# The sixth expert of a routed mixture, too, in products of two parts of each operand

## The chip, the cores and the metric

The kernel runs on one core of a Trainium2 chip. Its five engines work side by side, each through its own list of instructions: TensorE (PE; its weight loads are shown apart, as PEld), VectorE (DVE), ScalarE (ACT), GpSimd (POOL), and SyncE (SP), which here issues nearly all transfers between main memory and the core. The metric is device time of one launch in microseconds, median of several runs.

## The reference, cut to what matters

```python
x = attention(q, k, v)                    # 4 batches, 12 heads, 448 tokens, 64 wide -> [1792, 768]
logits = x @ w_gate                       # 8 experts
# greedy: in falling order of logits each token goes to its expert, 224 tokens per expert
for e in range(8):
    h = np.maximum(x[assigned == e] @ w1[e], 0.0)   # [224, 768] @ [768, 1024]
    out[assigned == e] = h @ w2[e]                  # [224, 1024] @ [1024, 768]
gate = 1 / (1 + np.exp(-(out @ w_gate2)))           # 768 -> 1536
final = (gate * (out @ w_val2)) @ w_out2            # 1536 -> 768
```

All of it is float32. The second, gated layer follows the experts.

## The kernel before, in words

Three stages follow each other: attention, the experts with the routing, the gated layer. The experts are worked in the order in which the routing closes them. A *phase* `ph` (0 to 7) is one round of the routing: it finds the next expert that is full, its number (`ei[ph]`) and the 224 rows that it gets (`ids[ph]`). `moe(ph, nxt)` then multiplies that expert; the sixth expert is `ph` = 5.

**One expert.** `xprep` turns the gathered rows with 12 TensorE transposes (L820). The first product has four chunks of `w1`, each 256 columns wide: 12 products of a 128x128 weight block with 224 columns, so 48 in all. The second product has four chunks of `w2` and also 48. A hidden chunk is taken out of PSUM by ScalarE (L862), and in a split expert its low part by VectorE (L864). All matrix products are issued at L778.

**Plain and split.** For a phase that isn't in `SPLIT` operands are float32 and each product is one matmul, which the trace shows as two records of PE. For a phase in `SPLIT` every operand has a high part (rounded to the type `fp32r`) and a low part (the rest), and a product is three matmuls: high·high, high·low, low·high (`prod` inside `moe`). The low part of the turned rows is made by L825.

**Weights.** Chunks are loaded in the order of use by `load_chunk` into a ring of 8 buffers, tile `w`. A chunk is fetched in two halves of 384 KB (`load_half`: L762 for `w1`, L768 for `w2`). A plain chunk takes one buffer, and the transfer writes into it, so that it can't start before TensorE has finished with what lay there. A split chunk takes two buffers. Its transfers go into one of four staging tiles, `raw`; then per half ScalarE writes the high part (L689) and VectorE the low part (L690). So a transfer into `raw` waits for a staging tile, and L689 and L690 wait for TensorE to leave the buffers.

**Routing.** `route()` runs beside the experts, one phase ahead of need or more. A phase is a chain of short steps between VectorE and TensorE. Six times VectorE compares (L498), TensorE counts with 14 short matmuls (L503), VectorE tests the counts (L514, tile `ge`), TensorE spreads them (L516), and VectorE narrows the search. Then come a prefix sum (L574, L577, read by TensorE at L580), the one-hot rows (L615), the count of the indices by TensorE (L619), and the indices themselves (L621, L622). SP stores them at L624 in tile `idx_d`, 224 words of 4 bytes each, and POOL gathers the rows of the next expert (L803). `tick` and `step` put these steps among the expert's matmuls at fixed places, by a count of the matmul time that has passed.

**What sets the order.** TensorE's order is that of the code. The lists of the other engines are laid out ahead of time by a scheduler that simulates the program; routing steps have priority. On the chip each engine works through its list.

**Weights of the gated layer.** They are float64 words in memory and are converted by a chain of ScalarE and VectorE steps (L83 to L94, tiles `cs`, `ca`, `sq`). The first two pieces of them are converted while the fifth expert runs.

The body of `load_chunk` for a split chunk:

```python
wh_, wl_ = wt(), wt()
for n in range(2):
    cc = slice(n * 768, (n + 1) * 768)
    raw = mo.tile([128, 768], F32, name="raw", bufs=4)
    load_half(kind, a, c, n, raw)
    nc.scalar.activation(wh_[:, cc], raw, AF.Copy)
    nc.vector.tensor_tensor(wl_[:, cc], raw, wh_[:, cc].bitcast(F32), op=OP.subtract)
```

Of the kernel before, what the change touches and what calls it, by code (L numbers as in the profile page):

```python
# [21 lines left out]
E = 8  # L22
# [8 lines left out]
def body(ctx: ExitStack, tc: tile.TileContext, q, k, v, moe_w_gate, moe_w1, moe_w2,  # L31
# [635 lines left out]
    for f in range(0, NF, 2):  # L667
        chunks += [("s0", 1, f), ("s1", 1, f), ("wo", 1, f)]

    SPLIT = (E - 2, E - 1)  # L670
    W = {}
    stream = {"next": 0}
    regs = {}
# [2 lines left out]
    def wt(dt=F32R):  # L676
        return mp.tile([128, CH], dt, name="w", bufs=WB)

    def load_chunk():
        kind, a, c = chunks[stream["next"]]  # L680
        if kind in ("w1", "w2") and a not in regs:
            regs[a] = nc.sync.value_load(ei[a][0:1, 0:1], min_val=0, max_val=E - 1)
        if kind in ("w1", "w2") and a in SPLIT:
            wh_, wl_ = wt(), wt()
# [125 lines left out]
    def xprep(ph):  # L810
        xs = XE[ph]
        sp = ph in SPLIT
        xx = mo.tile([128, KD, CAP], F32R if sp else F32, name="xx", bufs=2)
# [16 lines left out]
    def moe(ph, nxt):  # L830
        xx = XE[ph]
        hs_ = []
        sp = ph in SPLIT

# [239 lines left out]
```

## Time and profile before

| | us |
|---|---|
| median of 3 runs | 1130.82 |
| lowest, highest | 1128.95, 1131.06 |
| the profiled execution, its own time | 1130.21 |
| its span in the trace | 1128.4 |
| PE busy | 1076.9 (95%) |
| DVE busy | 699.1 (62%) |
| ACT busy | 439.5 (39%) |
| POOL busy | 270.2 (24%) |
| TensorE's granted clock, mean share | 0.979 |

Times in the trace are microseconds from the start of the span. The profiled execution's own time is 1.8 us longer than the span and 0.6 us under the median. Attention lasts to about 247, the opening of the routing to 283, the experts from there to 602, and the gated layer to the end. A busy share tells how long an engine had something in it, not that it decided the time; what decides is read from who waited for whom.

### The profile page before, as it was taken

How to read it: one execution, taken by the hardware profiler on the slowest of the kernel's cores; microseconds unless marked ns; L12 is line 12 of the kernel's file. 1: busy time of each engine (PE TensorE's matmuls, PEld its weight loads, DVE VectorE, ACT ScalarE, POOL GpSimd, SP SyncE). 2: the span in 40 equal slices, each digit the busy share in tenths (PEclk: the TensorE clock that was granted, in tenths of full speed). 3: DMA queues.
4: the chain of work that ended last, by engine and by line, in shares of the span. 5: the costliest groups of instructions: out<-in, count | busy, mean ns of one | idle time of the engine just before them, and what ended most of it. 6: DMA issues, size and time to landing. Idle time of an engine off the chain costs nothing.

```text
span 1128.4 us, 19849 instructions
## 1 busy us (share of the span) xinstructions
PE 1076.9 (95%) x7401; PEld 1020.8 (90%) x7401; DVE 699.1 (62%) x1980; ACT 439.5 (39%) x846; POOL 270.2 (24%) x371
## 2 busy tenths in 40 slices
PE   6999999982999999999999899999999999999997
PEld 6999999971899999999999799999999899899897
DVE  5777777766555556442557989878736515435535
ACT  4767677730111111123454465543414442322310
POOL 7333333300000000000000300000125746546522
PEclk9999999995999999999999899999999999999999
DMA  8556565525687667786747676655311521220212
GB/s 173 121 124 170 117 166 122 145 82 97 228 197 193 128 178 193 165 210 181 226 154 226 240 250 229 236 169 191 93 81 56 183 87 54 97 99 29 85 57 98
DMA packets 156991, 167.26 MB, mean 148 GB/s; under 512 B 74576, under 2 KB 140128, under 8 KB 156640
## 3 DMA queue, kind: packets, MB, share of 16 engines
q1 hardware_dynamic: 153472, 154.74, 46.1%
q0 software_dynamic: 2496, 11.04, 5.3%
q8 instruction: 58, 0.95, 0.4%
q10 hardware_dynamic: 928, 0.23, 0.1%
q14 instruction: 37, 0.30, 0.1%
HBM read 122.32 MB, written 32.64 MB: 137 GB/s over the span
## 4 chain that ended last, share of the span: by engine, by line
PE 90%; DVE 5%; issue 1%; DMA 1%; POOL 1%; ACT 1%; POOLq 0%; SPq 0%; ACTq 0%; DVEq 0%
PE g L778 67%; PE o L348 8%; PE w L328 4%; PE s L295 3%; PE s L296 2%; PE r L503 2%; PE w L257 1%; PE g L820 1%; DMA x_d<-x2f 1%; PE w L386 1%; PE w L369 1%; DVE ca L89 1%; DVE w L94 1%; DVE ca L92 0%; DVE hx L934 0%
## 5 line engine op out<-in xcount | busy, mean ns | idle before, releaser
L778 PE MATMUL g<-xq,w 128*128 128x448 f32 x1188 | 282.1, 367 | 0.0
L778 PEld LDWEIGHTS g<-xq,w 128*128 128x128 f32 x1188 | 222.7, 188 | 21.4
L778 PE MATMUL g<-w,hx 128*128 128x384 f32 x1008 | 181.6, 338 | 7.9 <-DVE hx L934 5.8
L778 PEld LDWEIGHTS g<-w,hx 128*128 128x128 f32 x1008 | 176.4, 190 | 12.0 <-DVE hx L934 8.3
L778 PE MATMUL g<-xx,w 128*128 128x224 f32 x768 | 151.4, 339 | 0.0
L778 PE MATMUL g<-hx,w 128*128 128x224 f32 x864 | 151.2, 331 | 0.0
L778 PEld LDWEIGHTS g<-hx,w 128*128 128x128 f32 x864 | 137.6, 191 | 2.5 <-issue 1.0
L778 PEld LDWEIGHTS g<-xx,w 128*128 128x128 f32 x768 | 134.9, 191 | 2.2 <-issue 0.2
L778 PE MATMUL g<-xs,w 128*128 128x448 f32 x432 | 124.7, 365 | 0.0
L742 POOL TENSOR_TENSOR w<-cs,w 128x384 fp32r<-128x384 f32 x84 | 84.2, 1024 | 121.4 <-ACT w L741 121.3
L348 PE MATMUL o<-vt,pt 112*112 112x65 f32 x960 | 106.3, 258 | 0.0
L348 PEld LDWEIGHTS o<-vt,pt 112*112 112x112 f32 x960 | 101.9, 178 | 0.0
L923 DVE TENSOR_TENSOR acc<-g,acc 128x384 f32<-128x384 f32 x140 | 75.3, 554 | 33.3 <-PE g L778 32.3
L298 DVE CUSTOM_DVE_ANT_0 sm<-s,mask 112x112 f32<-112x112 f32 (+1 forms) x192 | 78.4, 445 | 23.0 <-PE s L296 23.0
L306 ACT ACTIVATE sm<-sm,mn 112x112 f32<-112x112 f32 (+1 forms) x192 | 90.3, 522 | 5.1 <-DVE mn L298 5.1
L778 PEld LDWEIGHTS g<-xs,w 128*128 128x128 f32 x432 | 81.1, 188 | 6.2
L803 POOL DMA_INDIRECT xg<-x_d,ids x16 | 15.4, 962 | 296.3 <-DVE ids L622 105.4
L268 POOL CAST st<-hi 64x448 fp32r<-64x448 f32 x96 | 53.3, 556 | 133.4 <-ACT hi L263 122.8
L741 ACT ACTIVATE w<-cs 128x384 fp32r<-128x384 f32 x84 | 40.0, 518 | 92.4 <-PE g L778 48.7
L295 PE MATMUL s<-st,st 128*112 128x112 f32 (+1 forms) x192 | 62.2, 339 | 3.0 <-POOL st L268 2.6
L328 PE MATMUL w<-ident,sm 112*112 112x112 f32 x480 | 62.7, 261 | 0.1
L296 PE MATMUL s<-lo,qz 128*112 128x112 f32 (+1 forms) x192 | 56.5, 309 | 0.0
(214 smaller groups left out, 1450.0 us busy)
## 6 DMA issues: line engine op xcount, KB each, us to landing
w<-in_moe_w_dram SPq DMA_DIRECT2D x96, 384.0 KB, 6.6
raw<-in_moe_w_dram SPq DMA_DIRECT2D x32, 384.0 KB, 4.6
cs<-in_moe_w_gate_dram SPq DMA_DIRECT2D x12, 768.0 KB, 4.2
cs<-in_moe_w_val_dram SPq DMA_DIRECT2D x12, 768.0 KB
wsc<-ca SPq DMA_DIRECT2D x24, 384.0 KB, 4.7
cs<-in_moe_w_out_dram SPq DMA_DIRECT2D x12, 768.0 KB, 4.2
wsc<-w SPq DMA_DIRECT2D x12, 768.0 KB, 4.0
cs<-wsc SPq DMA_DIRECT2D x24, 384.0 KB, 3.1
```

The lines of the kernel that those rows point to most:

```text
L268: nc.gpsimd.tensor_copy(st[r, h], hi[r].bitcast(F32))
L295: nc.tensor.matmul(ss[j], qq[:, j, qs], kh[:, j, :w], start=True, stop=False)
L296: nc.tensor.matmul(ss[j], QZ[u % NZ][:, j, qs], kl[:, :w], start=False, stop=True)
L298: nc.vector.tensor_tensor_reduce(sm[:, j, :w], ss[j], mask[:, S - w:], op0=OP.add, op1=OP.min, scale=1.0, scalar=3.0e38, accum_out=mn[:, j ...
L306: nc.scalar.activation(sm[:, j, :w], sm[:, j, :w], AF.Exp, bias=mn[:, j:j + 1], scale=-1.0)
L328: nc.tensor.transpose(w[:P, n, :], sm[:, j, c * P:(c + 1) * P], ident[:P, :P])
L348: nc.tensor.matmul(o[:, n, j, :], pt[:, j * (i + 1) + c, :], vt[:, j, c, :], start=c == 0, stop=c == i)
L503: nc.tensor.matmul(c[:, :J], oha[:, tt_, :], cmps[2 * tt_ // T][:, tt_ % (T // 2), :J], start=tt_ == 0, stop=tt_ == T - 1)
L741: nc.scalar.activation(hi, src, AF.Copy)
L742: nc.gpsimd.tensor_tensor(lo, src, hi.bitcast(F32), op=OP.subtract)
L778: nc.tensor.matmul(o, a, b, start=first, stop=last_)
L923: nc.vector.tensor_tensor(ac, po[:, :384], ac, op=OP.add)
```

## The change

One line: the sixth expert (phase 5) joins the two that are split already.

```diff
-    SPLIT = (E - 2, E - 1)
+    SPLIT = (E - 3, E - 2, E - 1)
```

The names in the lists below are the lines and tiles that were described above; a count behind `x` stands for equal neighbours. On VectorE, inside phase 6 of the routing, while the fifth expert's first product runs: the second search's first compare (`cmp`) and its test (`ge`).

```order
 L535 SCALAR_TENSOR_TENSOR key_6780<-hs,th,lo_152 128x14
 L498 TENSOR_TENSOR cmp<-key_6780,jc_64_1024_93 128x448 x2
+L690 TENSOR_TENSOR w<-raw,w 128x768 x2
 L514 TENSOR_SCALAR ge<-r,rem_129 128x64
 L519 TENSOR_SCALAR jk,acc<-r 128x64
```

The two low parts of the sixth expert's first chunk now stand between the compare and the test.

On VectorE a little later, at the prefix sum of phase 6 (`sc`, `tot`), which stands among conversion steps of the gated layer (`ca`):

```order
-L87 TENSOR_SCALAR ca<-cs 128x768
+L690 TENSOR_TENSOR w<-raw,w 128x768
 L574 SCALAR_TENSOR_TENSOR sc<-chain,pr 128x28
+L690 TENSOR_TENSOR w<-raw,w 128x768
 L87 TENSOR_SCALAR ca<-cs 128x768
 L591 SCALAR_TENSOR_TENSOR rem_129<-e_6964,d_115 8x1
 L564 SCALAR_TENSOR_TENSOR jk_7037,na<-ob,n_107 128x8
-L88 SCALAR_TENSOR_TENSOR ca<-cs,ca 128x768
+L87 TENSOR_SCALAR ca<-cs 128x768
 L577 CAST tot<-sc 128x2
```

The second chunk's two low parts now stand ahead of `tot`, and one conversion step (L88) has moved behind it.

On VectorE from the end of phase 7 of the routing (`ids`) on, through the sixth expert, as it stands now; before, nothing stood between `o` and `c`, and no L864 belonged to this expert:

```order
L615 TENSOR_TENSOR o_80<-pm,colp 128x7x112 x2
L825 TENSOR_TENSOR xl<-g,xx 128x448 x3
L690 TENSOR_TENSOR w<-raw,w 128x768 x2
L621 COPY c_7174<-r 112x4
L622 SCALAR_TENSOR_TENSOR ids_147<-c_7174 112x2
L690 TENSOR_TENSOR w<-raw,w 128x768 x2
L864 SCALAR_TENSOR_TENSOR hx<-g,hx 128x448
```

The first L690 pair here is the sixth expert's fourth chunk, the second its fifth, and L864 is its first hidden chunk. After these rows a pair and an L864 take turns three more times (chunks six to eight, hidden chunks two to four), so that each hidden chunk's low part comes behind the split of a later chunk of weights. ScalarE's list (L689 and L862) alternates in the same way.

SP issues as many transfers as before. The four halves of the sixth expert's first two chunks stand at the same place, behind the last half of the fifth expert's `w2`, but go into `raw`; the third chunk's two halves follow at once, too, and the fourth chunk's come behind the read of `ei` of phase 6. The index store of phase 6 (`idx_d`) now stands between the sixth expert's fifth and sixth chunk, and that of phase 7 between its sixth and seventh. PE's list differs in the sixth expert alone: 96 products become 288 matmuls. POOL's list is the same.

## Rows read from the trace of the kernel before

**Rows 1.** The page's first part: busy us, share of the span, instructions.
```profile
PE 1076.9 (95%) x7401; PEld 1020.8 (90%) x7401; DVE 699.1 (62%) x1980; ACT 439.5 (39%) x846; POOL 270.2 (24%) x371
```
**Rows 2.** Waits of PE, 300 to 620 us: us in total, times, longest.
```profile
PE r L516 <- DVE ge L514: 0.3, 1, 0.3
PE r L619 <- DVE o L615: 0.2, 1, 0.2
```
**Rows 3.** Timeline of PE, experts six to eight: start us, us, engine, line, count.
```profile
498.99 2.43 PE L778 MATMUL g<-xx,w 128*128 128x224 f32 x12
501.25 0.49 PE L619 MATMUL r<-r,o 128*128 128x4 bf16 x14
517.58 15.30 PE L778 MATMUL g<-hx,w 128*128 128x224 f32 x80
536.75 0.43 PE L778 MATMUL g<-xx,w 128*128 128x224 f32 x1
552.98 13.56 PE L778 MATMUL g<-hx,w 128*128 128x224 f32 x120
570.23 0.28 PE L778 MATMUL g<-xx,w 128*128 128x224 f32 x1
```
**Rows 4.** Groups by line and shape: count, busy us, mean ns, idle before.
```profile
L690 DVE TENSOR_TENSOR w<-raw,w 128x768 fp32r<-128x768 f32 x32 | 29.3, 956 | 42.1 <-ACT w L689 40.4 <-PE g L778 1.6
L689 ACT ACTIVATE w<-raw 128x768 fp32r<-128x768 f32 x32 | 25.5, 839 | 29.8 <-PE g L778 15.6 <-DMA raw<-in_moe_w_dram 14.2
```
**Rows 5.** Timeline of all engines, phase 6: compare, count, test, spread.
```profile
466.82 0.62 DVE L498 TENSOR_TENSOR cmp<-key,jc 128x448 bf16<-128x448 f32 x1
...
468.10 0.57 PE L503 MATMUL r<-cmp,oha 128*128 128x64 bf16 x14
...
468.71 0.28 DVE L514 TENSOR_SCALAR ge<-r,rem 128x64 bf16<-128x64 f32 x1 [1.27 <-PE r L503]
...
469.35 0.19 PE L516 MATMUL r<-ge,sv 128*128 128x64 bf16 x1
```
**Rows 6.** Timeline of SP, the issues at the fifth expert's start.
```profile
455.09 0.33 SPq L624 DMA_DIRECT2D idx_d<-ids  x1
455.68 2.34 SPq L768 DMA_DIRECT2D w<-in_moe_w_dram  x4
```
**Rows 7.** Tile w, SP at 457.64 us: the last of those four halves, us to landing.
```profile
L768 SPq DMA_DIRECT2D w<-in_moe_w_dram x1: 373/373/373, 457.6 to 457.6; - x1
DMA to landing us min/median/max: 16.0/16.0/16.0
```
**Rows 8.** Busy time by stretch; the last three columns are granted clock, DMA share, GB/s.
```profile
455.00:464.00 9.00, 9.00 (x73) 8.57 (x72) 4.02 (x18) 1.26 (x3) 1.86 (x2) 1.00 0.67 41
516.00:524.00 8.00, 8.00 (x44) 8.00 (x43) 2.09 (x3) 2.67 (x6) 0.00 (x0) 1.00 0.56 67
524.00:527.00 3.00, 3.00 (x17) 3.00 (x17) 0.08 (x1) 1.77 (x3) 0.00 (x0) 1.00 0.97 338
```
**Rows 9.** Timeline of SP: the index store of phase 7.
```profile
509.06 1.41 SPq L624 DMA_DIRECT2D idx_d<-ids  x1
```
**Rows 10.** Timeline of ACT: the seventh expert's first two halves.
```profile
513.35 0.84 ACT L689 ACTIVATE w<-raw 128x768 fp32r<-128x768 f32 x1 [8.64 <-DMA raw<-in_moe_w_dram]
514.43 0.84 ACT L689 ACTIVATE w<-raw 128x768 fp32r<-128x768 f32 x1 [0.24 <-DMA raw<-in_moe_w_dram]
```
**Rows 11.** Timeline of PE in the gated layer: a wait.
```profile
634.84 1.01 PE L778 MATMUL g<-w,hx 128*128 128x384 f32 x2 [2.00 <-ACT hx L933]
```
**Rows 12.** Busy time by stretch, columns as in rows 8, soon after that wait.
```profile
637.70:641.70 4.00, 4.00 (x12) 4.00 (x13) 3.06 (x5) 3.16 (x5) 0.00 (x0) 0.50 0.79 269
```
**Rows 13.** Timeline of all engines, phase 6: the prefix sum.
```profile
480.17 0.94 DVE L88 SCALAR_TENSOR_TENSOR ca<-cs,ca 128x768 uint32<-128x768 uint32 x1
...
481.04 0.15 DVE L577 CAST tot<-sc 128x2 bf16<-128x2 f32 x1
...
481.31 0.17 PE L580 MATMUL r<-tot,before 128*128 128x2 bf16 x1
```

## The prediction

> **What bounds the kernel now.** I read the page's busy shares first: PE is busy for 1076.9 of the span's 1128.4 us [rows 1]. A busy share proves nothing by itself, so I read next who PE waits for in the experts. From 300 to 620 us there are two waits, together 0.5 us, both for a routing step of DVE [rows 2]. So PE's list sets the time there. What PE saves comes off the end, and any wait put into its list is added in full. The timeline of PE prices the experts, the groups by line price the new work of ACT and DVE, and the timelines of the single engines, together with SP's issues and the table of stretches, tell when the new work's inputs are there.
>
> **The change part by part.**
>
> *PE's products.* The sixth expert runs from 498.99 to 536.75, that is 37.76 us plain; the seventh, split, from 536.75 to 570.23, that is 33.48 us [rows 3]. Both have 96 products and 12 transposes. The sixth also has 14 matmuls of the routing, busy for 0.49 us [rows 3], of which I count 0.36 on the path. Split, it should take 33.84 us: **-3.9 us**. The single products agree: 40 plain ones in 15.30 us are 0.38 us each, 40 split ones in 13.56 us are 0.34.
>
> The Trainium skill ("FP8 and Floating Point Precision", section TensorE Precision Notes) has true FP32 as four passes through the array. Three products in place of four passes would then save a quarter of 96 x 0.38, or 9.2 us. The rows disagree, since a split product costs 0.88 of a plain one and not 0.75, and the rows decide.
>
> *More splitting.* The expert has 8 chunks, so 16 halves: 16 x 0.839 = 13.4 us more on ACT and 16 x 0.956 = 15.3 us more on DVE [rows 4], and on DVE also three L825 and four L864. Neither engine is full there, so the sum costs nothing by itself. What costs is where it stands. DVE works its list in order, and two places of that list are inside the routing, for which PE waits.
>
> The Trainium skill says of this ("TensorE: Matmul & The Clock Gate", the table ahead of its first section) that ScalarE's and VectorE's queues are strictly first in, first out, while TensorE's may pull weight loads ahead. If that didn't hold on DVE, the next term would vanish and the gain of 3.9 us would stand. No run here tests it by itself.
>
> *First place, the test `ge` of phase 6.* Before, the compare is issued at 466.82, PE counts at 468.10, `ge` runs at 468.71 for 0.28 us, and PE's L516 follows at 469.35 [rows 5]. Now two L690 stand ahead of `ge`. They need both halves of the sixth expert's first chunk in `raw`, and L689 of each. When do those arrive? SP issues them right behind the four halves of the fifth expert's `w2` that go out from 455.68 on [rows 6]. The last of these four is issued at 457.64 and takes 16.0 us to land, so until 473.6 [rows 7]. The reason is in the table of stretches: in the 9 us after the index store of 455.09 the DMA engines are 67% busy and move only 41 GB/s [rows 6, 8]. The same follows the store of phase 7, issued at 509.06 behind other transfers: 67 GB/s for 8 us from 516 on, then 338 GB/s [rows 8, 9]. There the gather of rows is not near, so I put it down to the store. It is in the changed kernel at the same place.
>
> At 338 GB/s a half (384 KB, 0.393 MB) takes 1.16 us. The seventh expert's first two halves came 1.08 us apart, too [rows 10]. So the two halves land at about 474.8 and 475.9. L689 of the second ends at 476.8, L690 at 477.7, `ge` at 478.0, and L516 starts at about 478.15 in place of 469.35: **+8.8 us** of PE waiting. Bounds: if the halves were there, L690 could start at 468.1, when PE leaves the second buffer; 2 x 0.956 and `ge` end at 470.3, and PE waits 1.1 us. If they come 2 us later than I think, it is 11. I take 8.8, since the landing of that half is a row and not a guess. Behind the wait on DVE are all later steps of the routing, and on ACT the fifth expert's hidden chunk, which nobody needs that early.
>
> *The clock.* In the gated layer PE waited 2.00 us [rows 11]; afterwards the granted clock was 0.50, 1.2 GHz, and stayed there through 4.0 us of dense work from 637.70 to 641.70 [rows 12]. So the long wait should drop the clock as well, and about 4 us at half speed lose **+2.0 us** (bounds 0 and 2.0).
>
> *Second place, the prefix sum of phase 6.* DVE has no pause there. `tot` starts at 481.04 for 0.15 us, and PE's L580 at 481.31, 0.12 us later than `tot` ends [rows 13]. Two L690 (1.91 us) now come ahead of `tot` and one L88 (0.94) falls behind it [rows 4, 13], so it comes 0.97 us later: **+0.85 us** of waiting (bounds 0 and 1.9).
>
> *Inside the sixth expert.* The seventh and eighth run through without a wait [rows 2], with the same pattern of loads. The sixth has two index stores among its loads, and the one of phase 7 stands just ahead of the seventh chunk. Count from the expert's start. The store leaves at about 7 us, behind the sixth chunk, which phase 6's store has already delayed; the stretch of few bytes lasts to 15 [rows 8]. The seventh chunk's halves, 1.16 us each and partly moved by then, land at 16 to 16.5. Two L689, the take-out of the third hidden chunk behind them (0.5) and on DVE L690 and L864 (0.6) end at 19.2. PE finishes the first product after 16.2 us [rows 3] and wants that hidden chunk four products later, at 17.8: **+1.4 us**. Bounds: 0, as in the seventh expert, and 5.2 if the stretch lasts 9 us as from 455 on, nothing gets through in it, and the clock falls once more. I take 1.4.
>
> *After the sixth expert* the lists are those of before and every load waits for PE to leave a buffer, so all of it moves along: 0.
>
> *Sum.* -3.9 + 8.8 + 2.0 + 0.85 + 1.4 = **+9.1 us**. Against the profiled execution's own 1130.21 us that gives 1139.3. The median of the runs is 0.6 higher, within their spread, so I say 1139.5. With all low bounds: -3.9 + 1.1 = -2.8. With all high ones: -3.9 + 11 + 2 + 1.9 + 5.2 = +16.2.
>
> **Rivals.**
>
> *The halves are there in time (not slower).* This rests on one arrival: the first chunk in `raw` before 468. For it: the transfers no longer wait for PE and are issued as early as 458. Against it: they queue behind a transfer that landed at 473.6 [rows 7]. Then the two places cost 1.1 + 0.85 and the sum is -2.0, about 1128.5. It turns from slower to faster when the arrivals move ahead by some 6 us.
>
> *No wait at all (faster).* If DVE's extra work also fitted into the 1.27 us that it sat idle ahead of `ge` [rows 5], and the slack at `tot` sufficed, the whole -3.9 would come through: 1126.5. Against it: two L690 take 1.91 us.
>
> *The arrival lies between.* With the chunk there at 470 to 472, PE waits 3 to 5 us, the clock may hold, and the sum is -2 to +2: about 1131.
>
> *The columns alone set a product's price.* Three products of 224 columns would then cost three quarters of a plain one, and the 96 would save a quarter of 96 x 0.38, or 9.2 us; with the waits the sum is about +4, without them -9. The split experts' rows speak against it [rows 3]. The passes of the skill's page, above, give the same.
>
> *The sixth expert starves.* If each of its later chunks waits for a store, PE waits several times and the clock stays low: over +16, above 1146. For it: two stores in one expert with half the lead in weights. Against it: chunks five and six are issued well ahead.
>
> That the change doesn't do what it says is out: PE's list has three matmuls per product there.
>
> **How the numbers follow.** Forecast 0.72 (1133 to 1146 by itself). In time 0.10, half of it faster, half too small to tell. No wait 0.06. In between 0.05, no change. Columns alone, without waits, 0.02. Starving 0.05. What a measurement of this kernel can tell from no change is 0.2%, 2.3 us. So faster 0.13, same 0.10, slower 0.77. The range from 1129 to 1146 leaves out about half of "in time", the faster cases and the starving: just under 0.2.
>
> **What would show it.** In the changed kernel's trace: L516 after the first count of phase 6's second search with a wait of about 9 us for `ge`; on DVE L690 waiting for L689, and on ACT L689 for the transfer into `raw`; granted clock 0.50 just behind; a wait of about 1 us at L580; the sixth expert about 33.8 us long apart from waits, and one wait for L864 early in its second product; from the seventh expert on, rows as before, only later. I am wrong if the first L690 of the sixth expert finds its data, or if its products don't take 0.34 us each.

## The result, and the profile after

The changed kernel takes 1138.58 us (median of 6 runs, 1135.9 to 1140.26), the kernel before 1131.18 us in the 6 runs beside it and ahead of it (1128.95 to 1132.03). The ratio is 1.0063, its 95% interval 1.0046 to 1.0080: 7.4 us slower. The profiled execution took 1138.94 us, its span is 1137.2.

PE's busy time in the page of the changed kernel stands against [rows 1]:

```profile
PE 1074.7 (95%) x7497; PEld 1018.2 (90%) x7497; DVE 718.0 (63%) x2003; ACT 453.0 (40%) x862; POOL 269.9 (24%) x371
```

PE is busy for 2.2 us less than before and ends 8.7 us later. So the loss is waiting, and the next view is that of PE's waits from 300 to 640 us (columns: total, times, longest), where before had 0.5 us in all [rows 2]:

```profile
PE r L516 <- DVE ge L514: 7.7, 2, 7.4
PE g L820 <- DMA xg<-x_d,ids: 1.1, 1, 1.1
PE g L778 <- DVE hx L864: 0.7, 1, 0.7
PE r L580 <- DVE tot L577: 0.6, 1, 0.6
PE g L778 <- ACT hx L862: 0.4, 1, 0.4
```

The second line is a wait for the second expert's rows, ahead of anything that the change touches. With it and with what went before, the fifth expert starts 2.19 us later than in the profile of before. In the twelve other profiles below that start lies 0.9 to 7.3 us later than there, with the order of work up to it unchanged (one of them has the kernel before's own split). So it is scatter between executions, and in all tables here shifts are counted from the start of the fifth expert.

PE's timeline shows the two places in the routing, and then the sixth expert's second product; to set beside [rows 3, 5, 13]:

```profile
470.29 0.57 PE L503 MATMUL r<-cmp,oha 128*128 128x64 bf16 x14
479.14 0.21 PE L516 MATMUL r<-ge,sv 128*128 128x64 bf16 x1 [7.43 <-DVE ge L514]
493.61 0.18 PE L580 MATMUL r<-tot,before 128*128 128x2 bf16 x1 [0.64 <-DVE tot L577]
527.49 1.50 PE L778 MATMUL g<-hx,w 128*128 128x224 f32 x12
529.42 0.37 PE L778 MATMUL g<-hx,w 128*128 128x224 f32 x1 [0.43 <-ACT hx L862]
530.52 12.21 PE L778 MATMUL g<-hx,w 128*128 128x224 f32 x107 [0.73 <-DVE hx L864]
```

What DVE and ACT did meanwhile (DVE's three rows first, then ACT's; the wait ahead of a row stands in brackets):

```profile
468.47 1.16 DVE L498 TENSOR_TENSOR cmp<-key,jc 128x448 bf16<-128x448 f32 x2
477.05 1.84 DVE L690 TENSOR_TENSOR w<-raw,w 128x768 fp32r<-128x768 f32 x2 [7.42 <-DMA raw<-in_moe_w_dram]
478.80 0.28 DVE L514 TENSOR_SCALAR ge<-r,rem 128x64 bf16<-128x64 f32 x1
```

```profile
476.17 1.73 ACT L689 ACTIVATE w<-raw 128x768 fp32r<-128x768 f32 x2 [10.54 <-DMA raw<-in_moe_w_dram]
```

PE had finished counting at 470.9. `ge` takes 0.28 us, but two L690 stand ahead of it in DVE's list, and they wait for halves that ACT could first touch at 476.17. SP's issues and the table of stretches (last three columns: granted clock, DMA share, GB/s) tell why these come late, as [rows 6, 8] did:

```profile
457.29 0.33 SPq L624 DMA_DIRECT2D idx_d<-ids  x1
457.88 2.34 SPq L768 DMA_DIRECT2D w<-in_moe_w_dram  x4
460.40 10.31 SPq L762 DMA_DIRECT2D raw<-in_moe_w_dram  x4
```

```profile
457.30:466.00 8.70, 8.70 (x72) 8.28 (x71) 3.89 (x16) 1.26 (x3) 1.86 (x2) 1.00 0.68 35
470.00:478.80 8.80, 1.70 (x21) 1.36 (x20) 1.75 (x2) 2.12 (x3) 0.00 (x0) 0.83 0.93 278
479.10:483.00 3.90, 3.86 (x17) 3.44 (x17) 1.35 (x6) 0.00 (x0) 0.00 (x0) 0.54 0.64 201
```

For 8.7 us behind the index store the DMA engines move 35 GB/s. In the second row PE is busy for 1.7 of 8.8 us; in the third, the dense work behind the wait, the granted clock is mostly 0.50, that is 1.2 GHz.

How far each event of PE has moved against before, in us, counted from the fifth expert's start (for each kernel the profiled execution; "first spread" is the L516 behind the late `ge`, "after search" the search's last L516, "prefix" phase 6's L580):

| kernel | first spread | after search | prefix | sixth starts | seventh starts | eighth starts | end | ratio of the runs |
|---|---|---|---|---|---|---|---|---|
| changed kernel | +7.6 | +9.3 | +10.1 | +9.6 | +7.5 | +7.3 | +6.5 | 1.0063 |
| e6_late: no stores in the experts | +1.2 | +1.2 | +2.0 | +1.6 | -2.3 | -1.1 | -2.8 | 0.9988 |
| e3_store: the same, another late place | +1.6 | +1.6 | +2.4 | +1.9 | -1.9 | -1.2 | +7.3 | 1.0048 |
| x2_double: one store twice | +15.7 | +17.2 | +18.0 | +17.5 | +17.1 | +16.9 | +16.9 | 1.0173 |
| e7_before_late: before without the stores | -0.1 | -0.1 | -0.1 | -0.1 | -0.1 | -0.1 | -2.5 | 0.9998 |
| p1_products: no low parts of weights | 0.0 | 0.0 | 0.0 | +0.5 | -2.8 | -3.0 | -3.3 | 0.9979 |
| e1_pool: four L690 on POOL | 0.0 | 0.0 | +5.4 | +5.2 | +5.8 | +6.8 | +7.0 | 1.0055 |
| e1a_pool_first: two L690 on POOL | +0.3 | +0.3 | +4.3 | +3.8 | +3.5 | +3.3 | +3.4 | 1.0036 |
| e9_tot: L690 behind `tot` | +0.1 | +0.1 | +0.1 | +6.5 | +4.8 | +5.0 | +5.5 | 1.0057 |
| e8_late_tot: e6 and e9 | +0.1 | +0.1 | +0.1 | +6.7 | +2.9 | +3.4 | +3.2 | 1.0049 |
| e2_behind: L690 behind the row numbers | -0.1 | -0.1 | -0.1 | +5.0 | +7.0 | +6.9 | +5.9 | 1.0082 |
| e6b_late_behind: e6 and e2 | -0.1 | -0.1 | -0.1 | -0.2 | +1.0 | +2.4 | +6.2 | 1.0000 |
| e10_pauses: e6, L690 in DVE's pauses | 0.0 | 0.0 | 0.0 | +0.1 | -3.8 | -3.3 | -3.1 | 0.9985 |

### The profile page after: what moved, and what is told of

The parts are those of the page before. It is cut to its first block, busy times and chain, and to the rows that moved or that the text cites. A ratio compares the mean times of both kernels' runs of the same rounds, so it can differ in the third digit from the quotient of the medians.

```text
span 1137.2 us, 20102 instructions
## 1 busy us (share of the span) xinstructions
PE 1074.7 (95%) x7497; PEld 1018.2 (90%) x7497; DVE 718.0 (63%) x2003; ACT 453.0 (40%) x862; POOL 269.9 (24%) x371
## 4 chain that ended last, share of the span: by engine, by line
PE 86%; DVE 5%; DMA 5%; POOL 1%; issue 1%; ACT 1%; SPq 0%; POOLq 0%; DVEq 0%; ACTq 0%
PE g L778 63%; PE o L348 8%; PE w L328 4%; PE s L295 3%; PE s L296 2%; DMA xg<-x_d,ids 2%; DMA raw<-in_moe_w_dram 2%; PE w L257 2%; PE r L503 1%; PE g L820 1%; DMA x_d<-x2f 1%; PE w L386 1%; PE w L369 1%; DVE ca L89 1%; DVE w L94 1%
## 5 line engine op out<-in xcount | busy, mean ns | idle before, releaser
L778 PEld LDWEIGHTS g<-xx,w 128*128 128x128 f32 x768 | 133.0, 193 | 10.1 <-issue 7.7
L690 DVE TENSOR_TENSOR w<-raw,w 128x768 fp32r<-128x768 f32 x48 | 44.2, 955 | 40.5 <-ACT w L689 33.0
```

Source lines behind the costliest of these rows:

```text
L778: nc.tensor.matmul(o, a, b, start=first, stop=last_)
```

## The experiments

The theory (A): PE loses time because low parts of weights stand in DVE's list ahead of routing steps, and their halves come late because an index store holds up the transfers. The rivals: the amount of new work on DVE and ACT (B), weights late because a split chunk takes two buffers (C), the gather or the bytes in place of the store (D), and lateness that costs wherever the low parts stand (D').

**Two halves of the cause: lateness.** Deferring the stores (the later runs use a place further on, `e6_late`):

```
- nc.sync.dma_start(idx_d[ph ...], ids[ph])
+ (nc.sync.dma_start(idx_d[ph ...], ids[ph]) if ph < E - 3 else None)
  ...
+ for ph in range(E - 3, E):          # e3: behind the last expert; e6: behind moe2a()
+     with tc.issue_after(...):       # e3: the last x2_d store; e6: the last converted weights
+         nc.sync.dma_start(idx_d[ph ...], ids[ph])
```

> The changed kernel, with the index stores (L624) of the last three experts issued only after the last expert instead of among its weight loads; in the experts all lists stay as they are, and the gathers of rows stay where they are. Theory A with the store as the cause of the late halves: the first chunk's halves land some 7 us earlier, at about 466 to 468; L690 find them, the wait for ge shrinks to 1 to 2 us (two L690 of 0.96 us), the clock stays full, the wait at tot stays (0.8), the wait inside the sixth expert (1.7) goes: about 1138.6 - 6 - 1.7 - 1.7 = 1129 us. Theory D (the gather of rows, or the sheer bytes of weights, hold up the halves): the wait for ge stays at 7 us or more and the time at 1138 us. Theory B: 1138.6 us.

> The changed kernel with the index stores of the last three experts issued late in the first gated layer (behind its last converted weights) instead of among the experts' weight loads; the lists of PE, DVE, ACT and POOL stay as they are in the changed kernel. The earlier form of this, with the stores right behind the last expert, lost 8.5 us in the gated layer and stood 1.2 us ahead of before at the eighth expert. Theory A (two L690 ahead of ge wait for halves that the store holds up): the wait for ge is 1.1 to 1.7 us, the clock holds, tot costs 0.6 to 0.8, the wait inside the sixth expert 0.6 or less: -3.8 + 1.5 + 0.7 + 0.4 = 1.2 us less than before (ratio 0.999), if the late stores hold up nothing; they stand ahead of the reads for the second gated layer, and if these are short of time it is up to 24 us more. Theory B (amount of work on DVE and ACT): 6 to 7 us more than before, as the changed kernel.

e3 1.0048 (1.0031 to 1.0064), e6 0.9988 (0.9975 to 1.0000). In the experts both did what A says, to a few tenths; over the whole e6 came out as A said (0.999), and e3 missed A's 1129 us. PE's waits in e6 from 440 to 640 us, and the stretch behind the place of the store, which a gather of rows still falls into:

```profile
PE r L516 <- DVE ge L514: 1.1, 1, 1.1
PE g L778 <- ACT hx L933: 0.9, 1, 0.9
PE g L778 <- DVE hx L864: 0.7, 1, 0.7
PE r L580 <- DVE tot L577: 0.6, 1, 0.6
```

```profile
460.50:466.00 5.50, 5.50 (x42) 5.32 (x42) 2.31 (x10) 0.72 (x2) 1.86 (x2) 1.00 0.64 209
```

209 GB/s in place of 35. The first of the four `w2` halves is issued at about the same moment in both, 1.3 and 1.2 us ahead of the fifth expert's start; ACT's first L689 starts 10.8 us after that, and 18.3 in the changed kernel. The last of the four lands 7.3 us after its issue, and 14.9 in the changed kernel. D is out: the gather and the bytes of weights are still there. B is out: DVE's and ACT's lists are those of the changed kernel. e3's gain was lost again in the gated layer: three stores in a row at 607 us, and PE waits 9.5 us there for a hidden chunk (1.9 in the changed kernel).

Of the 1.1 us that PE still waits for `ge`, 0.5 us are for the second half, which comes a little late even without the store:

```profile
475.06 0.96 DVE L690 TENSOR_TENSOR w<-raw,w 128x768 fp32r<-128x768 f32 x1 [0.48 <-ACT w L689]
```

The other direction, a second store:

```
+ idx_e = dram.tile([N, 1], I32, name="idx_e")
+ for t_ in (idx_d, idx_e) if ph == E - 3 else (idx_d,):
      nc.sync.dma_start(t_[ph ...], ids[ph])
```

> The changed kernel with the index store of the sixth expert (the one among the fifth expert's w2 loads) issued twice, the second time into a spare tensor; all lists but that one entry of SP stay. Theory A with the store as the cause: the stretch in which the transfers hardly move gets up to 8 us longer, the first chunk's halves land that much later, and the wait for ge grows from 7.6 to about 15 us: 1146 us. If the two stores overlap in the queues, the wait grows by less; with half an overlap 1142 us. Theory D (gather or bytes): 224 more words of 4 bytes are nothing beside 1.5 MB of weights, so 1138.6 us and a wait of 7.6 us. Theory B: 1138.6 us.

1.0173 (1.0155 to 1.0191), some 5 us above A's 1146 us (15 us above before). PE's wait for `ge`, the two rows of DVE that show it, and the table of stretches behind the stores of 460.62:

```profile
PE r L516 <- DVE ge L514: 12.3, 2, 6.2
```

```profile
476.93 0.25 DVE L514 TENSOR_SCALAR ge<-r,rem 128x32 bf16<-128x32 f32 x1 [7.46 <-remote]
488.45 1.85 DVE L690 TENSOR_TENSOR w<-raw,w 128x768 fp32r<-128x768 f32 x2 [9.14 <-DMA raw<-in_moe_w_dram]
```

```profile
460.60:470.00 9.40, 9.40 (x85) 8.85 (x84) 3.95 (x17) 1.26 (x3) 1.87 (x2) 1.00 0.83 26
470.00:477.00 7.00, 1.06 (x13) 0.81 (x10) 0.07 (x1) 0.00 (x0) 0.00 (x0) 0.73 0.86 41
```

The stretch of few bytes is twice as long. ACT's first L689 comes 27.0 us after the first store, 18.9 in the changed kernel: 8.1 us for 224 more words of 4 bytes. The first spread moves by 15.7 us, close to the 15 of the forecast, but not all of it at the wait for L690: 6.4 us come at the `ge` before, which DVE began 7.5 us after its last step for a reason that the trace calls only "remote". No other run has this, and it stays open.

As a control, the kernel before with the stores moved as in e6:

> The kernel before (fifth expert's successor plain) with the index stores of the last three experts issued late in the first gated layer, all other lists as they are. In the kernel before nothing waits for the transfers that the store holds up, so theory A: the same time as before within 0.5 us up to the eighth expert, and over the whole if the late stores hold up nothing; any difference behind the experts is the price of their new place and is to be taken off the other two runs. Rival: the store costs the kernel before something too, and taking it away gains over 1 us in the experts; then the gain of the other runs is partly not the change's.

0.9998 (0.9983 to 1.0013), no shift in the experts. So the store costs nothing where no routing step stands behind what it holds up. The store and the place cost 7.6 us together at the first spread; the place without the store 1.2 (e6), the store without the place nothing (e7, and e9 below).

**Two halves of the cause: the place in DVE's list.** DVE's work on these weights taken away altogether. This kernel leaves out their low parts and multiplies by the high part once more in their place, so its products are not the reference's; PE's list is the same:

```
- wh_, wl_ = wt(), wt()
+ wh_ = wt(); wl_ = wt() if a != E - 3 else wh_
  ...
+ if a != E - 3:
      nc.vector.tensor_tensor(wl_[:, cc], raw, ...)
```

> The changed kernel without the low parts of the sixth expert's weights: no L690 for its eight chunks and one buffer of the eight per chunk instead of two; the products take the high part twice, so PE's list stays the same to the instruction. This leaves out the low parts of these weights. ACT's L689 and the low parts of rows and hidden values stay. Theory A: no wait for ge beyond 0.3, none for tot, no half clock, and with the lead in chunks of before no wait inside the sixth expert: the whole gain of the products, -3.8 us, ratio 0.9966. Theory B (amount): ACT's 16 L689 stay, so something of the loss should stay too, ratio 1.000 or more. If a product's price were set by its columns alone the gain would be 9 us, ratio 0.992.

0.9979 (0.9969 to 0.9990), a gain of 2.4 us of the 3.8 that A gave; the profile's is 3.3. No wait at `ge` or `tot`, 0.5 us at the sixth expert's start (for the turned rows and their low parts), and the sixth expert 3.3 us shorter. ACT's part of the amount (B) costs nothing that can be seen. C is not told apart by this run, since a chunk takes one buffer here; e6 and e10, with two, speak against it.

The low parts moved to POOL:

```
- nc.vector.tensor_tensor(wl_[:, cc], raw, ...)
+ (nc.gpsimd if (kind, a) == ("w1", E - 3) and c < 2 else nc.vector).tensor_tensor(...)   # e1a: c == 0
```

> The changed kernel, with the four low parts (L690) of the sixth expert's first two chunks on POOL instead of DVE; every other list stays. Times of before and after are 1131.2 and 1138.6 us. Theory A (place and arrival: PE waits because two L690 stand ahead of ge, and two ahead of tot, in DVE's in-order list, and their halves come late): the wait of L516 for ge falls from 7.6 to under 0.3 us, the half clock behind it (1.7) and the wait of L580 for tot (0.8) go too, the wait inside the sixth expert (1.7) stays: about 1138.6 - 10.1 = 1128.5 us, faster than before by 2 to 4 us. Theory B (amount: 16 more L690 and 16 more L689 slow DVE and ACT as a whole): only 4 of 16 L690 leave DVE, so at most a quarter of the loss comes back, about 1136.5 us. Theory C (the weights themselves come late, since a split chunk takes two of the eight buffers): nothing is loaded earlier, 1138.6 us, and PE waits for weights instead of ge.

> The changed kernel, with only the two L690 of the sixth expert's first chunk on POOL; those of the second chunk stay on DVE ahead of tot. Theory A: the wait for ge (7.6 us) and the half clock (1.7) go, the wait of L580 for tot stays at 0.7 to 0.9 us: 1138.6 - 9.3 = about 1129.3 us. Theory B: an eighth of the loss at most, about 1137.5 us. Theory C: 1138.6 us. If the wait at tot came only from the late start of all that stands behind ge, it would go here too, and the time would be that of the run with all four on POOL.

1.0055 (1.0039 to 1.0071) and 1.0036 (1.0019 to 1.0053): the times that I gave for A were missed. The wait for `ge` did go (none in e1, 0.2 us in e1a), and the clock's fall behind it. But the clock fell at other places, for 3.4 us each, in e1a behind a wait of 2.1 us for `sat` (L549) and in e1 inside the sixth expert, and new waits came, in e1 these from 440 to 640 us:

```profile
PE r L580 <- DVE tot L577: 3.0, 1, 3.0
PE r L553 <- DVE sat L549: 2.0, 1, 2.0
PE g L778 <- ACT hx L862: 1.5, 1, 1.5
PE g L778 <- DVE hx L864: 1.5, 2, 0.7
```

POOL's timeline in e1, then DVE's in the same microseconds:

```profile
479.13 3.58 POOL L690 TENSOR_TENSOR w<-raw,w 128x768 fp32r<-128x768 f32 x2 [17.75 <-DMA raw<-in_moe_w_dram]
484.56 5.43 POOL L690 TENSOR_TENSOR w<-raw,w 128x768 fp32r<-128x768 f32 x2 [1.85 <-issue]
```

```profile
479.61 1.36 DVE L521 TENSOR_TENSOR th<-acc,cst 128x1 f32<-128x1 f32 x1
481.34 1.40 DVE L545 SCALAR_TENSOR_TENSOR new<-key,th,be 128x14 f32<-128x14 f32 x1
485.61 1.75 DVE L591 SCALAR_TENSOR_TENSOR rem<-e,d 8x1 f32<-8x1 f32 x1
488.25 1.76 DVE L577 CAST tot<-sc 128x2 bf16<-128x2 f32 x1
```

In the changed kernel these four take 0.16, 0.22, 0.14 and 0.15 us. Each of them falls into an L690 of POOL, which takes 1.8 to 2.8 us, while the steps between them keep their lengths. So DVE waits for POOL inside its instructions, and the four steps lie on the routing's chain. The Trainium skill ("SBUF — State Buffer", section SBUF: two separate sides) says that DVE and GpSimd share one pair of ports, held by one of them for a whole instruction, against DVE steps that read two operands from SBUF or run in a fast mode. The first three rows, with two operands each, agree with it; whether the fourth, a copy with one operand, runs in such a mode is not shown. Inside the sixth expert, too, e1 loses more than the changed kernel, 4.4 us against 1.7 (its length less the products).

The low parts kept on DVE, but further back:

```
+ with tc.issue_after(fins[E - 2].ins) if a == E - 3 else ExitStack():       # e2: phase 6's row numbers, L622
+ with tc.issue_after(<phase 6's tot, L577>) if a == E - 3 else ExitStack():  # e9
      nc.vector.tensor_tensor(wl_[:, cc], raw, ...)
```

> The changed kernel with its stores where they are, and the sixth expert's L690 behind the last step of phase 6's routing on DVE. Theory A: the halves come as late as in the changed kernel, but nothing of the routing stands behind them: no wait for ge or tot, no half clock there. What is left is -3.8 and the wait inside the sixth expert, 1.7 us or, with halves held in raw longer, up to 5: 0 to 2 us less than before. Unlike the run with POOL, DVE's small steps keep their 0.15 to 0.25 us. Theory B: as the changed kernel, 6 to 7 us more than before. Theory D' (the late transfers themselves, not the order on DVE): as the changed kernel.

> The same, and the sixth expert's L690 come on DVE only behind the last step of phase 6's routing (its row numbers), so none stands ahead of ge or tot. Theory A: the waits for ge and tot go as well, 3.3 to 3.8 us less than before (ratio 0.997). Rival: held back so far, the low parts of the first chunks come in one stretch of 6 x 0.95 us and the four buffers of raw halves stay full, so the sixth expert waits for weights or hidden parts: 1 to 4 us of that gain are lost. Theory B: 6 us more than before.

> The changed kernel with its index stores in their place and the sixth expert's L690 on DVE right behind tot (L577) of phase 6. The halves are then as late as in the changed kernel, but nothing that PE wants stands behind them. Theory A: the waits for ge (7.6) and tot (0.8) and the half clock (1.7) go; -3.8 and the wait inside the sixth expert (1.7, in other runs up to 3 with the clock) are left: 0.8 to 2.1 us less than before, ratio 0.998 to 0.9995. Theory D' (late transfers cost their lateness wherever the low parts stand): the wait turns up at the start of the sixth expert instead, as it did with the low parts behind the row numbers (4.9 us for xx), ratio 1.005 or more.

> The changed kernel with the last three index stores late in the first gated layer (as in the run that gave 0.9988 of before) and with the sixth expert's L690 on DVE right behind tot (L577) of phase 6's prefix sum: behind ge and tot, but 10 us earlier than in the two runs that held them back to the row numbers. Theory A: no wait for ge (1.3 there) and none for tot (0.8), the halves in raw are taken out in time for the sixth expert: -3.8 of products come through but for 0.4 to 1.4 us inside the sixth and seventh expert: 2.4 to 3.4 us less than before, ratio 0.997 to 0.998. Rival: the sixth expert waits as it did when they were held back to the row numbers (1.5 to 5 us): ratio 0.999 to 1.001.

e2 1.0082 (1.0060 to 1.0103), e6b 1.0000 (0.9986 to 1.0014), e9 1.0057 (1.0037 to 1.0076), e8 1.0049 (1.0031 to 1.0067). A's times, 0 to 3.8 us less than before, were missed in all four. All four are alike in one thing, and A asked for it: `ge` and `tot` come on time to 0.1 us, with the halves as late as ever in e2 and e9. All four lose the gain at a later place. In e2 PE waits 4.9 us for the turned rows (L823): ACT's list has two L689 ahead of them, whose halves could be issued only when DVE had emptied `raw`, and then stood behind phase 6's index store. ACT's rows:

```profile
501.64 0.84 ACT L689 ACTIVATE w<-raw 128x768 fp32r<-128x768 f32 x1 [2.01 <-DMA raw<-in_moe_w_dram]
503.52 0.84 ACT L689 ACTIVATE w<-raw 128x768 fp32r<-128x768 f32 x1 [1.04 <-DMA raw<-in_moe_w_dram]
504.27 1.39 ACT L823 ACTIVATE xx<-g 128x448 fp32r<-128x448 f32 x3
```

In e6b, without the store, the sixth expert starts on time, but PE then waits 1.5 us for the rows' low parts (L825), which stand behind the delayed L690, and the clock falls to 0.50 for over 6 us: the expert takes 5.1 us longer than in e10. In e9 and e8 six L690 stand between `tot` and the one-hot rows L615, and PE waits 4.8 us for these, with and without the store (e8's row):

```profile
PE r L619 <- DVE o L615: 4.8, 2, 4.3
```

So D', that lateness costs wherever the low parts stand, is right in its outcome for these places, but not in its cause: e8 has no late halves and the same wait. What counts is whether the work that is put between two steps for which PE waits fits the slack there. The last run takes that literally: one L690 in each of two pauses of DVE, the next four behind L615.

```
+ with tc.issue_after(fins["c"][n - 2] if c == 0 and kind == "w1" else ones[E - 2].ins) if a == E - 3 ...:
      nc.vector.tensor_tensor(wl_[:, cc], raw, ...)    # fins["c"]: the last compare of each level of the search
```

> The last three index stores late in the first gated layer, and the sixth expert's L690 on DVE put where the trace of before has pauses: the two of the first chunk singly behind the compares of the second and third level of phase 6's second search (DVE pauses 0.89 and 0.91 us there, an L690 takes 0.95), those of the next chunks behind L615 of phase 6, for which PE waits at L619, with four in a row ahead of phase 7's tot. Theory A (what counts is what stands in DVE's list between one step that PE waits for and the next, and whether it fits the slack there): no wait over 0.3 us at ge, tot and L619 of phase 6; four L690, 3.7 us, against some 3.2 us of slack ahead of phase 7's L580: up to 0.6 there; inside the sixth and seventh expert 0.5 to 2. In all 1.2 to 3 us less than before, ratio 0.9973 to 0.999. Rival: the sixth expert's low parts then run late once more and a wait of 2 us or more turns up at its start or in its second product: ratio 1.000 or more.

0.9985 (0.9966 to 1.0005). DVE's two L690 in their pauses, each with the `ge` behind it:

```profile
478.19 0.95 DVE L690 TENSOR_TENSOR w<-raw,w 128x768 fp32r<-128x768 f32 x1
479.16 0.25 DVE L514 TENSOR_SCALAR ge<-r,rem 128x32 bf16<-128x32 f32 x1
481.37 0.95 DVE L690 TENSOR_TENSOR w<-raw,w 128x768 fp32r<-128x768 f32 x1
482.35 0.25 DVE L514 TENSOR_SCALAR ge<-r,rem 128x32 bf16<-128x32 f32 x1
```

Nothing moves up to the sixth expert (+0.1), which then gives its full 3.8 us. 0.5 us are lost in the seventh expert. The profile ends 3.1 us ahead of before, the ratio stands for 1.7 us (the two medians lie 1.05 apart), and the interval reaches to no difference. No version here beats the kernel before by more than its measurement can tell, except the one that leaves the low parts out.

## Why the prediction was right, step by step

The time (1139.5 forecast, 1138.58 measured) and the waits at their places came as told. The change came out smaller than its sum: +9.1 forecast, 7.4 by the medians, 6.5 in the profile. That the two times lie only 0.9 us apart is in part the scatter of the medians. The terms, from the profiles:

| term | forecast | measured | read from |
|---|---|---|---|
| PE's products | -3.9 | -3.84 | e10, sixth expert without a wait: +0.06 to -3.78 |
| first place, `ge` | +8.8 | +7.6 | first spread |
| the clock behind it | +2.0 | +1.7 | first spread to after search |
| second place, `tot` | +0.85 | +0.80 | after search to prefix |
| inside the sixth expert | +1.4 | +1.66 | its length, -2.17, less the products |
| after it | 0 | -0.9 | seventh expert's start to the end |

The measured terms add to 7.0; 0.5 us were given back between the prefix sum and the sixth expert, of which 0.2 are PE's earlier wait at L619 [rows 2]; the sum is the profile's 6.5. The medians say 7.4.

**Products.** The price of a split product from [rows 3] held to 0.1 us. The rival that columns alone set it would have made the sixth expert 9 us shorter; it is out.

**First place.** It came out 1.2 us smaller: L690 was done at 476.7 on the clock of before, not at 477.7 as added up from the landing of the last `w2` half [rows 7] and two halves of 1.16 us. Most of that is the landing, 14.9 us after the issue in the changed kernel and 16.0 in the row of before. The mechanism is shown from both sides: without the store 1.2 us are left, near the lower bound of 1.1 that the prediction set for halves that are there (0.5 of them are the late second half, so that this bound was a little high), and with two stores 15.7. The rule of the Trainium skill ("TensorE: Matmul & The Clock Gate", the table ahead of its first section) that VectorE's queue is strictly first in, first out now has runs for it: in the changed kernel `ge` has its counts at 470.9 and starts at 478.8, behind the L690; in e9 the halves are as late, no L690 stands ahead, and `ge` is on time.

**Clock.** It fell to 0.50 behind the wait of 7.4 us and cost 1.7. In e6, with a wait of 1.1 us, it stayed at 1.00. That a long wait drops the clock, as the prediction took from one wait of 2.00 us [rows 11, 12], is no rule by itself: in e1 it stayed at 1.00 behind a wait of 3.0 us for `tot`, and in e6b it fell behind one of 1.5. The stretches behind these three waits (e6, e1, e6b; third column from the end):

```profile
476.30:480.30 4.00, 4.00 (x34) 3.82 (x34) 2.14 (x11) 0.00 (x0) 0.00 (x0) 1.00 0.54 174
490.10:494.10 4.00, 4.00 (x22) 4.00 (x23) 3.97 (x10) 0.66 (x3) 0.00 (x0) 1.00 0.62 170
503.00:509.00 6.00, 6.00 (x41) 5.93 (x42) 2.40 (x5) 0.00 (x0) 0.00 (x0) 0.51 0.74 209
```

So the term came true at this wait, but the rows before could not make it sure.

**Second place.** 0.80 in the changed kernel and again 0.80 in e6; the two L690 cost the same with and without the late halves, as the sum had it.

**Inside the sixth expert.** PE waits behind 12 matmuls, four products, as worked out, for the third hidden chunk; there are two waits and not one, 0.4 us for ACT's L862 and 0.7 for L864. The prediction's 17.8 us doesn't follow from its rows: 16.2 and four products of 0.34 are 17.6, or 17.9 with the 0.36 of the routing. That the stores cause the waits is shown by e6: it has none in the sixth expert (one of 0.7 us for L864 stands in its seventh, which takes 1.2 us longer than before).

**After it.** The zero was wrong by 0.9 us. In the gated layer the stretch at half clock is 3.4 us long (646.5 to 649.9), against 6.8 before (634.9 to 641.7). I had expected every row there as before. This stretch differs between executions of the same lists (the control e7 gains 2.4 us in that layer with a median that says none), and I tested nothing on it.

**The rivals.** "The halves are there in time" was priced at -2.0; e6, which nearly makes it true, stands at -2.3 to -1.1 in the experts, and its runs at 0.9988. "No wait at all" was put at -3.9; e10 shows -3.8 at the seventh expert. "Starving" did not happen.

What the prediction did not see is that there was no simple way out: it treated the two places as the price, while behind each of them the next routing step stood with as little slack. Each of the four moves to a later place on DVE found such a step or the sixth expert's own rows, and only the one into DVE's pauses (e10) didn't.

## What to carry to other kernels

A helper's work has two prices: its duration, which a half idle engine hides, and its place in a list that is worked in order. For the second, look for the steps that the bounding engine waits for, the slack ahead of each, and the arrival of what the new instruction reads; a late operand is charged in full to whatever stands behind it. If the work is moved, the same sum has to be made at the new place, on every engine whose list it enters, and for the buffers that it now holds longer.

## What the runs showed of the hardware

- One store of 224 words of 4 bytes (0.9 KB) leaves the DMA engines at 35 GB/s for 8.7 us, and two leave them at 26 to 41 GB/s for 16.4. Weights issued behind one come 7.5 us later (e6 against the changed kernel), behind two another 8.1 us. With a gather of rows but no store the first 5.5 us of that stretch have 209 GB/s. The words themselves are soon gone: in the changed kernel's DMA packets 240 of the 245 of 4 bytes start within 1 us (458 to 459), and what crawls are the reads behind them, 1536-byte packets that take 65 ns in the median and up to 6.7 us here (0.7 at most in the same stretch of e6). The Trainium skill ("DMA: Bandwidth & Descriptors", section Specifications) asks for 512 bytes or more per transfer for full rate, below which the engines read, change and write back. That says slow for the store itself; that large reads queued behind it hardly move as well is what these runs add.
- An L690 takes 0.95 us on DVE and 1.8 to 2.8 on POOL, and while POOL works on it some of DVE's smallest steps take 1.4 to 1.8 us in place of 0.2.
